# A conformer block on one core: a new order of the instruction blocks and new PSUM banks, from a re-timing in which ScalarE's operations end later

## The chip, the cores and the metric

The kernel runs on one core of a Trainium2 chip. The metric is the device time of one execution in microseconds (us). A core has five engines that run their own instruction streams in order and meet only through semaphores: TensorE (PE in the profile; PEld is its weight load), VectorE (DVE), ScalarE (ACT), GpSimd (POOL) and SyncE (SP, which here only issues DMAs). Matrix products land in PSUM, which this kernel uses as eight banks of 512 fp32 columns.

## The reference

The input x has shape (2, 4000, 144): two sequences of 4000 tokens. The reference is one conformer block:

```python
h = layernorm(x);  x = x + 0.5 * (silu(h @ w_ff1a) @ w_ff1b)        # 144 -> 576 -> 144
h = layernorm(x);  q, k, v = split(h @ w_qkv)                        # 4 heads of 36
p = softmax(q @ k.T * 36**-0.5);  x = x + (p @ v) @ w_o              # full attention, 4000 x 4000
h = layernorm(x) @ w_pw1;  h = h[:, :144] * sigmoid(h[:, 144:])      # gated linear unit
c = depthwise convolution of h along the tokens, 5 taps
x = x + silu(c) @ w_pw2
h = layernorm(x);  x = x + 0.5 * (silu(h @ w_ff2a) @ w_ff2b)
return layernorm(x)
```

Nearly all of the work is the attention: 2 x 4 x 4000 x 4000 exponentials.

## The kernel before, in words

**Tiling.** The 8000 tokens are cut into 16 chunks of 500, eight for each sequence. The keys of a sequence are cut into 62 tiles of 64 and one of 32. One attention tile is one chunk of queries against one tile of keys for all four heads: a 128 x 1000 block of scores in two neighbouring PSUM banks. There are 16 x 63 = 1008 such tiles.

**One attention tile.** `emit_S` (line 1783) puts the scores on TensorE: eight 64 x 64 matmuls over 500 columns into a pair of banks out of the six banks 0 to 5. `emit_exp` (line 1797) then lets ScalarE take the exponential of all 1000 columns at once and write it as bf16 to one of 15 SBUF buffers (PT); with that the pair of banks is free again. `emit_O` (line 1866) multiplies the result with the values and adds it up in banks 6 and 7. For 190 of the 1008 tiles `dve_tile` (line 1811) does the exponential on VectorE with integer arithmetic: two operations read the scores from PSUM, each freeing one bank, and three more finish the tile in SBUF.

**The work around it.** Each chunk also goes through a front part (layer norm, first feed-forward in `ff_tile` at line 1208, the q, k and v projections) and a back part (`epilogue`, output projection, gated unit, convolution, second feed-forward, last layer norm and the store, in `post2` at line 1629). Their PSUM results come from the same six banks. Layer norm statistics are taken on VectorE, the power -0.5 on GpSimd, the normalised rows mostly on GpSimd, and they are transposed by VectorE and by DMAs through a scratch tensor `rows`. Inside the attention, silu is made of a tanh on ScalarE (TH) and a product on VectorE (HT, U, SW). The first 40 us or so and the last 40 us are without the full stream of attention tiles: there the chunks' own chains of dependent steps stand alone.

**What sets the order.** A planner in the kernel (class `Rec`, with the scheduler `Sched` and `pick`) first records all operations in an order that comes from an estimate of their durations. It is the same in both kernels. Operations that one call records on one engine are a block. Then `Rec.reorder(ORDER)` (line 281, called at line 2115) moves the blocks: for each of the five engines the table `ORDER` (line 38) has one letter for each block, which says by how many places it moves up or down in that engine's queue. `PLACES` (line 111) holds one digit for each PSUM tile: the bank, or the first of the pair, which it uses. `Rec.place` reads it. After that, `reorder` works out which tile of a bank follows which in TensorE's order, and makes the first matmul of the later one wait for the readers of the earlier one. So both tables act on waits, not only on positions. `Rec.replay` (line 409) issues everything; all instructions therefore have line L419 in the profile, and only their tiles tell them apart.

The moving itself is these lines of `reorder`:

```python
shift.append(c - 45)
...
at[i + shift[i]] = blk
...
lines[e] = [o for blk in at for o in blk]
```

Of the kernel before, what the change touches and what calls it, by code (L numbers as in the profile page):

```python
# [39 lines left out]
        "PPPPPPPPQOPPPPROQNPPQRPQLPPRPTPUPNIZOVOKVVL~OOKOK~OUHINSNLMMMOPNOJSOOL[I[KMYMKOGRNJHFKOOOE^NNN_dMKLM"  # L40
        "nXMJ@LJMFMYGaJNKMJhLLLLljKKKKKKWKMMWNKK`BJJJQRecHFSIGKH]QKMRGKPMJJMMQTNPNXTRSUJUJJJSLPMPPQUQQNKOTOOR"
        "OQLPPPPPYOOPN[NNNOMfRNLYULMIMOS^KIMOJNaNNQMNHPPaUOMQNYKPSPPQUSVV^QQ^_Q5<@QCPMKIMNNTQMSMNSNUOYQKMMOQQ"
        "^MSOORNOPPCOORPZP^O]OOO[OCNOQEHMUJNNTOMR[MQWXMPMMNNDMPXSNNZMMTMMMTMPLMPP]OOOOQQNUKNOMQMP]WNOMPNVKYPN"
        "JNQHNOOPQQQMPPQOPUP]MNNNOOTNNOMNWOPPMPNOW]VNN[MMHMKYMMQ]YKI`JLQYJJKV[KHMJTLJOJPMQORPVMQNYMN]MN[bLLLL"
        "LMNLPRPKWOYFMNOVNOHXXMKOLNNNN[[_MMMTLLTKKKLJOOPRP`MO_OMNOMPQLLMRMMMPPPQOSYP[MOOISOLNPPIPSPTOLRNNWPNO"
        "QQMMPUQRN[QQQRJFPPPPJQQSPPKQQNPPPPVPPQOPVXOOPNDNPRROSVSYNFWMPYUPNDPJFPNPTOPYOLOPNQ[NLNRPMRLNNOPhUNZM"
        "MMNLNNPMMWYLPNZKNLMF[LPPSLVINLNOMWQNYPYPLQHKOSNORPGPPPS[OOLOOPPYLNNNVOMNOM^QMNTOO_KMMNOMPPLPNQOYL]RY"
        "LMKLMMPLY]KLNNQXMRXSLI[MDObNOENPMMNSNNQMMWNNNOSVNiKZNNQOTFNNOMXXUMMMM?TLLIYMQXXLLMMQZMJJ`ORLMUMKQYNL"
        "INPMMUVNLNOMYPMOORNNRUNKPNO_ROQLSSKMQMKPROLPSOORNOSOOOTVNNNNSNTMTMNNOVXNOMORLSNVXIMSYLMKLN^XYNLMNHMM"
        "WLLMXMNYMOLNNXMNXMMVMM[SLJLLZN^OLNNJUbLLLQNLPRGNNOOOPNRNOPPPeOOOOPSOOORROf`OPNO^@QDLJLMOLTKLTMTRKGMQ"  # L50
        "QNUOPNROYYPZOHNbILLLLbTLLSLLLLPLM_M[MMMMMcMMMMNLMOdZMNNNNIMMMMXMNNVOMKMMZNOUaMMMQMM]^HOMKNNNJZMKM[LM"
# [31 lines left out]
    "dve": (
        "PUO[VM~P6~P6~P)~P6ILIKKLDKMJQRJJJKIKQKKLJKMKOLJWOILJHLJNQNPHFGNNNJMMMMBMWOIKIMINLMNOODNDPSPLORCFVSWC"
        "JDJSIOMBREEMKNCMMMMFNNJMMMMMMNLOPSPROLPPRPNPQOQOQQQMQOQQNPQQNQOPPQOPPQOPPPQOROOPROQVQOYPNOPROSPXURVQ"
        "UU;JNIQQSSSOSQRSSZRSSSKRVQUJ=OO)PROQNPRPRSLPRPQJQOPPPUOPNPQ`VPVOVOMEULFNKNRMRPQQQQIQOPQOQOSOORNTNOPN"
        "QOPQOPPQOQOPPPRPNPROQRMQRPQRPTPPPRPVVPNPSOLQQQQQQ5PPVPPPPPQRHQQQLPPPPPPPPQOPPPPPPPPPROSNPNPPPQSQSLSO"
        "RJQQLQQQQQQQQHPPROSPPTRPNQGQOPQOUQOPLQNRPNPQORUNNOOQNSOOTRUOMTOOPFPQOPPPPPPQQRRRKMRPNPQOPPPPPPPPPPQR"
        "PRPQQQHQOPWOPSOSKTLVOSNUNQMDOPPROOSOPNSQO^PjOOOSNNNCMNTMPLMNTNNNNNOOOPROOROOPRPQQRPJPRSNNQNPQOQOPQOQ"
        "OYRNNNYNOMNSOLRMULQNNOTPPMOQOQOPQOPPPSOPNSOSNPQLPPPPPPPVOOOOOXNOOROQNKUOOOOQNQOPPTTPNLNPPPPPPPPPPQSP"  # L90
        "PLQOPPP]OOOOOOOOOOOOQOQOPQOQOROOPQOWOPNOOOORPNPSPNSSPRSJTJWMRSLLRLMPTRNNQQLQOPPPPPPPPPQQSMPNPRPSPPQJ"
        "PPPPPQQNPQOQQNQOROOPQOPPPRPNPPPQQNPPPPTOOOOPQOPRPNQOQQRSOKQNQOSOOQNQRNOPQOSQRMMPPPPPROQNQOPPPPPQOPPP"
        "PQRPQRRORPQFPPPPPPPPPWPNPNOOOUPNOPNQSNSNNSNORNUQMPMOPROOROVNOOOPQMPPPPPPXQNQMQUNQNSOUQQUCOJOOPPQQNQO"
        "PPUPNOOOPPQRPQQRJQTPLOOTOOOOPPPQVNOQTMQNSQTNTFNNQNQOPPQQNPQOPPPQOQORPSPLOTOOOORORNQSMSNTRPRJRPIROQNQ"
        "OPTQNNTNOOSNSNNOUOOOOOPPPPPPROOROOQOQUROQSUSTGOHKPPPPPQOPQOQOPPQOPPROOQOPPPPPPPPPQRPUPPSORTRPRSUURXS"
        "=KQAQRNQQEPPPPPPPQOQOSOSOhTPMPRMSEOOKOPPPPPPROGNOPPPQRNRNOPQQQMPPPPPQQNQQNQQQQQKQQQRVOXOHOOLOOQNRPNP"
        "PPPPPPPSOOWNSNNQMUQKSOOQJQUN^PhLNKOPPKOKNNNPPMOOOOOOOOQQQRRKNPRPRPSQOQTPTODNRNQNQQUPLPROTRPWMXSNPSQW"
        "RZQUFOSDO7KOPPPTOOSOTOPPIPPPQOPPPPPPTPQMQMPQOPQQNQQRRORRRUQRPUWTQNRSCTRPRRRRDQQRPSPRSQR[RTQNPREO~NKO"
        "RNaNOOOPQMNQYNOPNPTQFNJPRRNNPPPPQOPQOPUPPPPSQOVVFNNNNNPPROOPPPPPROQNPPQQNPPRORPUPTQINLPPQOQOPPPPQOQQ"
        "RMTPPROUQRPFLQRNOPPROOUOXNNNUMNVWL[PRVIGPIOINQNPQQRTUSOITJPKOPSQS`PQQRHRSSTVSWWGRGW<FHMWWMVLLMTMKLO"  # L100
    ),
    "pool": (
        "PPPPPPPROOPPPSOPNPQQQQQQJPPPPPP_PPPPPJOOPQ[NKTMMOMNOSNUMNSNRNTKVNVMPLMPMROQTMOOTVMNNNOQTMOOQXMOOOTNN"
        "OMPPQOPPUOQNNOPPQOPQQNROO"
    ),
    "sp": (
        "PPQOPPPPQOPPPPPPPPPPPPPPWPWMNNNOPLPPPPPPQOPPPPPQRNOPPPPPQOPPQOPPPPPPPPPPPPPPPPPPPPPPPTOPNYNOWNNNNNNN"
        "VOWNNNNPMOPVOZNOMNNOOSNNNPPZOPNOOOOOOOPXOOOOOPPQLPPPPPPQO"
    ),
# [2037 lines left out]
```

## Time and profile before

| | us |
|---|---|
| median of 3 runs | 875.85 |
| lowest and highest | 875.37, 875.96 |
| profiled execution, its own time | 875.47 |
| its span, first to last instruction | 873.7 |
| TensorE busy | 844.9 |
| VectorE busy | 825.3 |
| ScalarE busy | 845.2 |
| GpSimd busy | 294.8 |

Three engines are busy for 94 to 97% of the span, so the share of busy time alone does not name the bound. Two things help in reading it. Operations on ScalarE overlap: the next one starts before the last one has written its result, so busy time can hide short delays, and the distance from start to start tells more than the duration. And TensorE's busy time holds pipelined matmuls with modelled ends, so a busy TensorE may have room.

### The profile page before, as it was taken

The page shows a single profiled execution, that of the slowest core. Times are in us where ns is not written, and L with a number is a line of the kernel's source. Part 1 is how long each engine was busy: PE and PEld are TensorE (multiplying, and loading weights), DVE is VectorE, ACT ScalarE, POOL GpSimd, SP SyncE. Part 2 cuts the span into 40 slices and gives each one's busy share as a digit, 9 for nine tenths or more (in the row PEclk, how much of TensorE's full clock was granted, in tenths as well). Part 3 has the DMA queues.
Part 4 walks back from the last instruction along what each step waited for, and adds up shares of the span by engine and source line. Part 5 has one row for each costly group of instructions (what it writes and reads, how often), then busy time and mean ns, then how long its engine had stood idle before and what let it go on. Part 6 is the DMA issues. An engine that isn't in the chain of part 4 may idle for free.

```text
span 873.7 us, 27060 instructions
## 1 busy us (share of the span) xinstructions
PE 844.9 (97%) x11419; PEld 385.8 (44%) x11419; DVE 825.3 (94%) x1821; ACT 845.2 (97%) x1098; POOL 294.8 (34%) x573
## 2 busy tenths in 40 slices
PE   8999999999999999999999999999999999999996
PEld 6543444334444434443444444445434433444466
DVE  8978999999999999999989999899999999999987
ACT  6799999999999999999999999999999999999985
POOL 6650450341325141152211552621414413022433
PEclk9999999999999999999999999999999999999999
DMA  4221101121121020212001120110111011001111
GB/s 100 51 57 32 24 17 43 35 66 31 27 53 39 16 51 11 44 22 48 21 4 29 24 56 17 31 29 16 38 31 25 20 31 21 18 15 37 25 29 35
DMA packets 114353, 28.82 MB, mean 33 GB/s; under 512 B 101090, under 2 KB 114230, under 8 KB 114230
## 3 DMA queue, kind: packets, MB, share of 16 engines
q1 hardware_dynamic: 112646, 26.39, 13.9%
q8 instruction: 90, 1.47, 0.7%
q10 hardware_dynamic: 1584, 0.69, 0.3%
q14 instruction: 33, 0.27, 0.1%
HBM read 13.44 MB, written 13.61 MB: 31 GB/s over the span
## 4 chain that ended last, share of the span: by engine, by line
ACT 65%; PE 20%; DVE 11%; POOL 3%; issue 1%; POOLq 0%; ACTq 0%
ACT PT L419 60%; PE PS L419 20%; ACT TH L419 5%; DVE PT L419 4%; DVE ST L419 2%; DVE XN L419 2%; POOL XN L419 1%; DVE X L419 1%; POOL RS L419 1%; DVE HT L419 1%; DVE RS L419 0%; DVE AN L419 0%; DVE U L419 0%; DVE KT L419 0%; DVE XT L419 0%
## 5 line engine op out<-in xcount | busy, mean ns | idle before, releaser
L419 ACT ACTIVATE PT<-PS 128x1000 bf16<-128x1000 f32 (+1 forms) x818 | 751.6, 1050 | 3.4 <-PE PS L419 2.8
L419 PE MATMUL PS<-QT,KT 64*64 64x500 bf16 x3968 | 419.4, 384 | 12.2 <-ACT PT L419 7.4
L419 PE MATMUL PS<-PT,VA 64*37 64x500 bf16 x4728 | 406.5, 372 | 1.8 <-DVE QT L419 1.0
L419 DVE TENSOR_SCALAR PT<-PS 128x500 int16<-128x500 f32 x380 | 250.7, 670 | 7.5 <-PE PS L419 5.7
L419 PEld LDWEIGHTS PS<-QT,KT 64*64 64x64 bf16 x3968 | 124.6, 104 | 230.4 <-ACT PT L419 130.3
L419 POOL TENSOR_SCALAR RS<-ST 125x4 f32<-125x4 f32 x130 | 38.3, 295 | 473.8 <-DVE ST L419 467.2
L419 PEld LDWEIGHTS PS<-PT,VA 64*37 64x37 bf16 x4728 | 142.4, 96 | 94.9 <-issue 14.1
L419 DVE TENSOR_SCALAR PT<-PT 128x1000 uint16<-128x1000 uint16 x380 | 154.7, 421 | 2.3 <-PE PS L419 1.0
L419 POOL TENSOR_SCALAR XN<-X,RS 125x144 bf16<-125x144 bf16 x260 | 144.9, 587 | 9.6 <-DMA out_dram<-XN 1.5
L419 DVE TENSOR_TENSOR PT<-PT 128x1000 bf16<-128x1000 bf16 x190 | 127.6, 675 | 0.8
L419 ACT ACTIVATE TH<-PS 128x500 bf16<-128x500 f32 (+3 forms) x194 | 102.3, 550 | 5.2 <-PE PS L419 5.2
L419 POOL TENSOR_TENSOR RS<-RS,NHALF 125x4 f32<-125x4 f32 (+2 forms) x93 | 93.9, 1013 | 33.6 <-DVE RS L419 28.1
L419 DVE SCALAR_TENSOR_TENSOR HT<-TH,PS 128x500 bf16<-128x500 bf16 (+1 forms) x135 | 81.2, 614 | 8.4 <-ACT TH L419 7.8
L419 PE MATMUL PS<-XT,WA 128*128 128x500 bf16 (+4 forms) x288 | 75.6, 368 | 3.4 <-DVE PT L419 0.8
L419 DVE BATCH_NORM_STATS2 ST<-X 125x6 f32<-125x288 bf16 x160 | 65.8, 447 | 1.6 <-DMA X<-in_x_dram 1.2
L419 DVE SCALAR_TENSOR_TENSOR X<-PS,X 125x288 bf16<-125x288 f32 x128 | 56.7, 450 | 4.9 <-PE PS L419 3.6
L419 PE MATMUL PS<-WB,HT 128*125 128x144 bf16 (+1 forms) x640 | 52.8, 230 | 0.6 <-ACT HT L419 0.2
L419 PEld LDWEIGHTS PS<-WB,HT 128*125 128x125 bf16 (+1 forms) x640 | 44.4, 136 | 13.9 <-issue 4.3
L419 PEld LDWEIGHTS PS<-XT,WA 128*128 128x128 bf16 (+1 forms) x288 | 21.4, 98 | 36.4 <-issue 10.3
L419 POOL COPY U<-U 128x2 bf16<-128x2 bf16 (+1 forms) x54 | 12.2, 266 | 56.2 <-DVE U L419 56.2
L419 DVE STREAM_TRANSPOSE XN<-XN 128x320 f32<-128x320 f32 x54 | 27.0, 501 | 4.0 <-POOL XN L419 4.0
L419 PE MATMUL PS<-U,DG 128*128 128x250 bf16 (+6 forms) x204 | 27.8, 263 | 0.1
(95 smaller groups left out, 521.0 us busy)
## 6 DMA issues: line engine op xcount, KB each, us to landing
rows<-XN SPq DMA_DIRECT2D x216, 40.0 KB, 2.0
XT<-rows SPq DMA_DIRECT2D x56, 128.0 KB, 2.0
rows<-AN SPq DMA_DIRECT2D x60, 40.0 KB, 2.0
X<-in_x_dram SPq DMA_DIRECT2D x15, 140.6 KB
XTQ<-rows SPq DMA_DIRECT2D x26, 70.3 KB
out_dram<-XN SPq DMA_DIRECT2D x13, 140.6 KB
XT<-rows SPq DMA_DIRECT2D x56, 16.0 KB, 1.9
out_dram<-XN SPq DMA_DIRECT2D x3, 70.3 KB
```

The costliest lines, as they stand in the source:

```text
L419: ins = getattr(eng, o.name)(*o.a, **o.k)
```

## The change

Both tables are replaced: `ORDER` and `PLACES`. All other lines are the same; so are all instructions, their shapes and their engines. The new tables come from a re-timing of the whole schedule in which ScalarE's operations end later than was assumed for the tables before, by what the trace shows.

Against the order before, on TensorE 8637 of 11419 instructions stand at another position (10 places away on average), on ScalarE 178 of 1106 (its DMA issues counted), on VectorE 1118 of 1821, on GpSimd 417 of 569, and 160 of SyncE's 466 DMA issues. Of 1724 PSUM tiles 254 are in another bank or pair.

The diff, cut to the first lines of some tables:

```diff
 ORDER = {
     "pe": (
-        "PPPPPPPPQOPPPPROQNPPQRPQLPPRPTPUPNIZOVOKVVL~OOKOK~OUHINSNLMMMOPNOJSOOL[I[KMYMKOGRNJHFKOOOE^NNN_dMKLM"
-        "nXMJ@LJMFMYGaJNKMJhLLLLljKKKKKKWKMMWNKK`BJJJQRecHFSIGKH]QKMRGKPMJJMMQTNPNXTRSUJUJJJSLPMPPQUQQNKOTOOR"
...
+        "PPPPPPPPQOPPPQOSPNOPQRPQLPPRPSPSQNI[XNOMQVLyLPI~OYKINRNLMMOOLOPNSOOH[J[KLYNKOHRNLHHKPNP@VOOOYdNLMNo["
+        "MKAMKMHLZLbIMIMIbLLLLiZJKKKKKXKNNXcGK^BKKKT[fMHHQKFHKfRLMSFLOMKQMMSLNNNXUMMXLLPMKSNNNPPUQRPMKSSNNUPV"
...
     "dve": (
-        "PUO[VM~P6~P6~P)~P6ILIKKLDKMJQRJJJKIKQKKLJKMKOLJWOILJHLJNQNPHFGNNNJMMMMBMWOIKIMINLMNOODNDPSPLORCFVSWC"
...
+        "PQQXZL~P)~P1~P5~P6KKKKKKDKKMKLOKKKMRJKKLJKMKOLJSMIMKHLJROMNHHHLNNJMMMMFMWOIKIMINLMOOODNDPRPLQSBFWSXC"
...
 PLACES = (
-    "3054320451505435202310543130213550204405323242301405230054110122532155431241204124012410314032034023"
...
+    "0410325144131405212310543130013550014415323302142105230054110123532155431241204124012410124032034023"
...
```

More of the change, by code (lines that the diff above doesn't have):

```diff
@@ new lines @@
+        "LMKPQRL[PPPPJOOOOOOPPROXNOOSNNNRTOPROQVTOOOOASOOQNXTWMNLZLOZUPNIPNDQO]UOPTOLBQNKOOROSQMNUOOOP]MO[NNN"
+        "NNTMOLLUYKOMOR]KXTZKURMKEGJKScMNQMQWWOLPHLNRMOROFPPPQSPPLPPQQZMOOPNOVNNNTMNN_PMZUMMMNLNYKNLP[UJTYNKK"
+        "HLXORL[RHKMMQWMTXNLIZMJNaMMYMOLLMYMMXLM[MMMNREMiQYMMPNZFMMNLXVKLLLLU^LLOGLQX[LLMMMPLPKaSULLPMKZMSNLM"
+        "NLQaTKKNOMPPMOOPQMRUNKPNOdQOQLPTRKOMKOPNOOXNNPMOQNNPXRNNNOPNUNZNNNNaPNOKOQLPMS]_OTTINHKQWNDIMNVOLOWN"
+        "NNTNN]MMOOO`NNVNNKMMYTMKNLXM]JMOOKX]RLJPMKVXGLNUKLLNTMQNNPeObNNORNNNQQNYaNOMN^?`CJJPMJUMJLUKPTKHMQQM"
@@ new lines @@
+        "WOPNOO[[RVNNJ[GLLLL[WKMULLLNXJLZMQMMYLMdMMMMPMMOdXMMMOMKMMMMXXMMYMMJNKRJN^VLOMQMMM^XOMKMMNYNNKN[MMRa"
+        "LLLNWMMMMYSLLLWbLPHMXTMGNKMTLXL[KLLcTMK]ZMJRGbKOLZIMMRAORKSMCLNPPRR_NLOOOPNWNOVLMMMMSUMUMMN`bLMbMMMM"
+        "MMMMNLNNPNYOGNWXNLOLNKROQKYaNOPNKQOLLOQQNQOXP]GNNOPNSXNNGOLOOOPXOOOOOOWOMWPNXKMMOZLOOLQQ[LLOMPPMeQdN"
+        "KPNPdMNNNNhQL?K_MIMHNINNKUNTVIKMKOHWOOOOVSYLSXKLTYKELY^KIMMMMNcMM_MMMMNOMSbMKMKLMXLNRMMeLLNO^JehLLRM"
+        "KIOYJbIFK`JGQIKKK[MaDKKLLcKLQNKKNNNNNSNNNNSYNOKSNN]NLNOOTPMPQKL]QQN[QJPMOPIMNOOPPhOPRMOPROWNTOMN`RTA"
@@ new lines @@
+        "OPPPPPPPROOPPSUNNNOQQMPPPPPPPQOQOPQOPPPPPPPPPPQOPPPPPPPPPPPQOPPPPPPPPPPQOPPPPQOQOPPPPRPNPQOPPQOQOQOQ"
+        "OPPRPNQOPPPPPPPPPPPPPPPPPPPPPPPPPPPPPPQRNOPRPQMPPPPPPPQQNPPPPPPPPPPPPPPPPPQOPPPPQOPPPPPPPPPPQOQOPPPP"
+        "PPPQOQOPPPPPPPPPPPPPPPPPQOPPPPPPQOPQQNPPPPPPPPPPPPPPPPPPPPTOOPNPPPPPPPPPQQNPPPPPPPPQOPPPPPRPNPPPPPPQ"
+        "OQOPPPPPPPPPPQRNOQOPPPPPPPQOPPPPPPPPPPPPQOPPQOPPPPPPPPPPPPPPPPPPPPPPPPPPPPPPPPPPPPPPPPPPPPPPPPPPPPPP"
+        "PPPPPPPPPPPPPPPQOPQOPPPPPPQOPPSOOTNPNRPRX_JMPMOLQMMOVNNOMOSNOOQOPQSPSOKOPSTTMNLNPPXQOPPKOOQN"
@@ L104 @@
[L104 removed]
+        "PPPPPPPQOPPPPSPNOPPPPQQQMQOPPPP[OOOOOSNNNPaLSQNLYLNNSMRLLTKWJNSXLOLPKOSNPMRUNPPTQJMOPQTNOOOQXNPPMPPP"
+        "QKPPPPPPSOOOPROOROOPROQN"
     ),
     "sp": (
[L107 to L108 removed]
+        "PPQOPPPPQOPPPPPPPPPPPPPPWQVMMNNOQLPSOOOPPQOPQOPQSNOOPPPPQOPPROOQOPPPPPROOPPPPPQOQOPPPVOPNWNNVMNNNNOP"
+        "UOWNNNNPNOPUOTNOMNPPPUOOOOOYQQMMOOOOOPPUYNNNNNOOOOPPPPQQN"
@@ new lines @@
+    "0245042504250235042504250425042504250425042504243023502430342035301430254320452042042504240525053205"
+    "2405420532052450240524052504250425042505250424053205240452203404203103215541240314210412041204131043"
+    "1034205320530515301030153502350523024302430243014301430243023501340243034203420134031340142034120402"
+    "1402140214021402140134143134021402140214021401340104312042104310431043104012430145301140124240214204"
+    "1214021402140210420041204120412041202423003423502431043024302421342503034021402142104214124021402140"
@@ new lines @@
+    "2140214021401340214020412040214031041204120412140134013402140204120402141124021402015240250425042052"
+    "4035023505240243010402342034120524120412040214020412041204120412412411034013402143425301503510351341"
+    "0401401342035320340134013402140120430253205301530153015301301035024310043214031530130104320430243014"
+    "1350235024302430243103502350230232042402340234203410431340135301530153015031503513513214301530134031"
+    "0431410420411043104301352035013403104310412043134013403104120412041204120431040214120423502430342024"
@@ L130 @@
+    "2034203420342034302402340234034030343421053103410430234022402504240524025040254214302430420425052024"
+    "3502350524042020420552054204520225043504320524052042505240524020532504523042321420040342034203420340"
+    "2532043104203420243024202430243024024310341042304302401530240324023203502350243024303240214021421412"
+    "0412041200412142043104024012411340104021401240210143502045312346410441340065523032142105143240214533"
+    "554032042015135102146143"
 )
```

113 lines of the change are left out of this document (41 added, 72 removed).

## The prediction

> **What bounds the kernel now.** I read the busy times first, then the chain of work that ended last, then the busy time by stretch.
>
> ```profile
> span 873.7 us, 27060 instructions
> ...
> PE 844.9 (97%) x11419; PEld 385.8 (44%) x11419; DVE 825.3 (94%) x1821; ACT 845.2 (97%) x1098; POOL 294.8 (34%) x573
> ...
> ACT 65%; PE 20%; DVE 11%; POOL 3%; issue 1%; POOLq 0%; ACTq 0%
> ```
>
> ```profile
> core 0: us, PE busy (x) PEld busy (x) DVE busy (x) ACT busy (x) POOL busy (x), PEclk, DMA share, GB/s
> 0.00:60.00 60.00, 55.55 (x612) 33.77 (x613) 52.02 (x152) 47.44 (x82) 41.83 (x94) 0.97 0.31 70
> 60.00:836.00 776.00, 758.48 (x10463) 327.28 (x10462) 742.79 (x1565) 772.59 (x955) 238.79 (x454) 1.00 0.14 30
> 836.00:868.00 32.00, 30.91 (x346) 24.77 (x346) 28.92 (x101) 24.06 (x61) 12.88 (x25) 1.00 0.10 26
> 868.00:873.70 5.70, 0.00 (x0) 0.00 (x0) 1.57 (x6) 1.13 (x3) 1.35 (x2) 0.62 0.17 47
> ```
>
> The second row is the attention: ScalarE is busy for 772.59 of 776 us, VectorE for 742.79, and 65% of the chain runs over ScalarE. The first and third rows, the start and the last three chunks, leave ScalarE idle for 12.6 and 7.9 us; there the chain is VectorE's and TensorE's.
>
> ScalarE's busy time is not its shortest time, since successive operations overlap. A stretch of its time order shows the distance from start to start:
>
> ```profile
> 413.49 2.87 ACT L419 ACTIVATE PT<-PS 128x1000 bf16<-128x1000 f32 x3
> 416.14 0.69 ACT L419 ACTIVATE TH<-PS 128x500 bf16<-128x500 f32 x1
> 416.61 6.50 ACT L419 ACTIVATE PT<-PS 128x1000 bf16<-128x1000 f32 x7
> 422.96 0.63 ACT L419 ACTIVATE TH<-PS 128x500 bf16<-128x500 f32 x1
> ...
> 424.31 0.45 ACT L419 ACTIVATE TH<-PS 128x250 bf16<-128x250 f32 x1
> 424.61 1.05 ACT L419 ACTIVATE PT<-PS 128x1000 bf16<-128x1000 f32 x1
> ```
>
> Three exponentials take 416.14 - 413.49 = 2.65 us, 0.883 us each, where nothing holds them. The next seven take 6.35 us, 0.907 each: 0.17 us of waiting that busy time hides. A 500-wide tanh takes 0.47, a 250-wide one 0.30. The groups of ScalarE between 60 and 836 us are:
>
> ```profile
> L419 ACT ACTIVATE PT<-PS 128x1000 bf16<-128x1000 f32 x782 | 724.8, 1059 | 2.6 <-PE PS L419 2.0
> L419 ACT ACTIVATE TH<-PS 128x500 bf16<-128x500 f32 x109 | 68.0, 638 | 0.8 <-PE PS L419 0.8
> L419 ACT ACTIVATE PT<-PS 128x500 bf16<-128x500 f32 x15 | 9.9, 663 | 0.0
> L419 ACT ACTIVATE TH<-PS 128x250 bf16<-128x250 f32 x20 | 9.3, 465 | 0.0
> L419 ACT ACTIVATE TH<-PS 64x125 bf16<-64x125 f32 x15 | 4.4, 296 | 0.0
> L419 ACT ACTIVATE TH<-PS 80x125 bf16<-80x125 f32 x13 | 3.8, 289 | 0.0
> L419 ACT ACTIVATE KT<-PS 128x500 bf16<-128x500 f32 x1 | 0.6, 615 | 0.0
> ```
>
> At their shortest distances: 782 x 0.883 = 690.5; the 125 operations of 500 columns x 0.47 = 58.8; 20 x 0.30 = 6.0; the 28 small ones at 0.12 (their mean less the 0.17 by which an exponential's mean of 1.059 exceeds its distance) = 3.4. Together 758.7 us. So 776 - 758.7 = 17.3 us, 2% of the time, is all that any order can win on ScalarE here; the profile's page counts 3.4 us of it as idle, the rest hides in the overlap.
>
> [...]
>
> **The change, part by part.** No instruction is added or removed, and ScalarE's own order hardly moves. What can change is how late the scores come, what TensorE's queue holds ahead of them, and how VectorE is fed. I counted this in the two orders.
>
> *Room before ScalarE's operations.* For each one fed by TensorE I take the last ScalarE operation whose end TensorE must see before the scores, and the TensorE work from that waiter to the end of the scores. Room is ScalarE's work in between less that work and less 0.28 us for the signals. TensorE's price is from these rows:
>
> ```profile
> 400.99 0.38 PE L419 MATMUL PS<-QT,KT 64*64 64x500 bf16 x4
> 401.20 0.38 PE L419 MATMUL PS<-PT,VA 64*37 64x500 bf16 x4
> 401.58 0.11 PEld L419 LDWEIGHTS PS<-QT,KT 64*64 64x64 bf16 x4 [0.48 <-ACT PT L419]
> 401.58 0.41 PE L419 MATMUL PS<-QT,KT 64*64 64x500 bf16 x4
> ```
>
> Four packed matmuls go in 401.20 - 400.99 = 0.21 us. (The last two are scores whose weight load waited 0.48 us for a bank of ScalarE, with the rest of the queue behind it.) Under 0.3 us of room had 102 of 946 operations before and have 87 after, 15% fewer: the intended effect is there. Its price lies between 15% of all 17.3 us (-2.6) and 0. Visible waits for scores are 2.0 + 0.8 = 2.8 us, and 15% of them is -0.4. I take -0.4: some 550 operations stand at 0.3 to 0.4 in both orders, and most of the hidden 13.9 us must be spread over them in pieces of hundredths.
>
> *Banks.* The pair of scores reuses the banks of the exponential two places before in 545 of 818 tiles, and in 540 after. In one case (at about 505 us) it now follows directly on the exponential before it, where none did. Then scores cannot run under that exponential: the last row prices four of the eight matmuls at 0.41, so with the signal +0.5 us; ends 0 and +0.6.
>
> *Feeding VectorE.* The same count for VectorE's operations fed by TensorE, with its own releases: under 0.3 us of room had 183 of 793, and have 234 after, 28% more. These are its waits for TensorE between 60 and 836 us:
>
> ```profile
> DVE PT L419 <- PE PS L419: 6.7, 19, 0.7
> ...
> DVE X L419 <- PE PS L419: 3.2, 9, 0.9
> ...
> DVE QT L419 <- PE PS L419: 1.5, 3, 1.2
> DVE RD L419 <- PE PS L419: 1.5, 4, 0.6
> ...
> DVE VA L419 <- PE PS L419: 1.1, 3, 0.7
> ```
>
> 28% of 14.0 us is +3.9. It costs nothing if VectorE's idle 33.2 us of the 776 cover it. They do so only where the chain is on ScalarE, and 35% of the chain is not: +1.4. But a late VectorE operation also holds its bank, and the scores for ScalarE stand behind the next user of that bank on TensorE's queue. That speaks for all of it. No row lies nearer to one of these two, so I take their middle, +2.6, and keep 0 and +3.9 as ends.
>
> *GpSimd and SyncE.* GpSimd's copies at the chunk edges move past whole groups of layer norm work, some by 100 us in the trace's terms. They cost nothing as long as the convolution that reads them comes later still, which it does in the new order; GpSimd's own waits are for work to arrive:
>
> ```profile
> POOL RS L419 <- DVE ST L419: 467.2, 41, 42.5
> ...
> PEld PS L419 <- DMA XT<-rows: 1.4, 4, 0.5
> ```
>
> Without that cover TensorE would stand behind a convolution. The 160 moved DMA issues pass layer norm rows and loads of x; TensorE waited 1.4 us in all for such data, so 0, with ends of -1.4 and +1.4.
>
> *The start.* Five clears of VectorE move into the gap before x lands, and TensorE swaps projections of the first two chunks. The first row's clock of 0.97 over 60 us is 1.8 us of lost clock; a filled or a new gap is worth that much, so I take 0 between -1.8 and +1.8.
>
> *The end.* From 836 us on, VectorE's order of the last three chunks is mixed anew (some steps by 10 us). It is busy for 28.92 of 32 us, so its work sets the length; its idle 3.1 us bound the gain, and I let as much more be the loss. Only the last steps can be read:
>
> ```profile
> 868.75 0.17 DVE L419 TENSOR_SCALAR RS<-ST 125x2 f32<-125x2 f32 x1
> 868.84 0.71 DVE L419 TENSOR_SCALAR XN<-X,ST,RS 125x144 bf16<-125x144 bf16 x2
> 869.74 0.16 DVE L419 SCALAR_TENSOR_TENSOR RS<-ST,RS 125x2 f32<-125x2 f32 x1 [0.20 <-POOL RS L419]
> ```
>
> ```profile
> 869.00 0.71 POOL L419 TENSOR_TENSOR RS<-RS,NHALF 125x2 f32<-125x2 f32 x1 [0.36 <-DVE RS L419]
> ```
>
> ```profile
> 869.94 0.90 ACT L419 ACTIVATE XN<-X,RS 125x144 bf16<-125x144 bf16 x2 [1.71 <-DVE RS L419]
> ```
>
> Now the last statistics (868.92) go through GpSimd to 869.71, VectorE's 0.16 and ScalarE's 0.90: 870.84. After, the half that ends last is normalised by VectorE itself: 0.08 + 0.70 for GpSimd and 0.71, from the same 868.92 as the work before it is the same: 870.4. That is -0.4, between -3.1 and +3.1.
>
> **The sum.** -0.4 + 0.5 + 2.6 + 0 + 0 - 0.4 = +2.3 us, on the profiled execution's 875.47 (span 873.7 and 1.8 around it): 877.8. That execution is 0.4 us under the median of 875.85; against the median I forecast +0.2%.
>
> **The rivals.** A measurement of this kernel can tell about 0.2% (1.75 us) from no change.
>
> *Faster: VectorE's idle time covers its waits.* Then +2.6 falls to 0 and ScalarE keeps its gain. For it: 65% of the chain is ScalarE's, and VectorE's 33.2 us. Against: 35% is not. Halfway between the small and the full gain on ScalarE (-1.5), with half of the start's 1.8 and the -0.4 of the end, it gives -2.8: 872.7; at the ends 870.7. It decides once less than about 0.3 us of VectorE's added waits reach the chain.
>
> *No change.* If ScalarE's 0.927 (724.8 / 782) were its shortest distance, a new order could win nothing, and the new waits would be hidden under it: 875.5. The 0.883 speaks against it. [...] It is also what comes out if gains and losses cancel.
>
> *Slower by the end alone.* VectorE's mixed order lets it run dry in the last three chunks, since a step of one half now stands ahead of a ready step of another: its idle time there doubles, +3.1, and the attention stays as it is: 878.6. For it: six halves share one queue. Against: TensorE is busy for 30.91 of 32 us there and feeds all of them.
>
> **How the numbers follow.** Slower by VectorE's feeding 0.33 (877.8; its own range 877 to 883, with the new waits, the end and the start all at their costs), slower by the end 0.12, faster 0.33, no change 0.22. The first and third are close; I hold the first for likeliest to come out, by the larger of the two changes in the counts (28% more against 15% fewer). So slower 0.45, within 0.2% 0.22, faster 0.33. The lowest sum of the ends is 875.5 - 2.6 - 0.4 - 1.8 = 870.7, the highest 875.5 + 0.6 + 3.9 + 1.8 + 3.1 = 884.9; 871 to 883 leaves out no more than 2 in 10.
>
> **What would show it.** Right: between 60 and 836 us the sum of VectorE's waits for TensorE grows from 14 to about 18 us, ScalarE's waits for scores stay near 2.8 us or fall a little, the stretch of the attention ends about 2 us later, and the last statistics are normalised by VectorE. Wrong: VectorE's waits grow and the attention ends no later (they were covered), or the distance of the exponentials falls from 0.927 by more than 0.003 (2.3 us over 782), or the time moves before 60 or after 836 us.

## The result, and the profile after

The changed kernel takes 881.75 us (median of 5 runs, 879.46 to 882.41), the kernel before 875.72 in the same session (875.04 to 875.96): a ratio of 1.0063, 95% interval 1.0047 to 1.008. So it is slower by 6.0 us where +2.3 was forecast, and its runs spread over 2.95 us where those of before spread over 0.92. The profiled execution is one of 881.75 us.

The page's lines on the span, the busy times and the shares of the chain, for the changed kernel:

```profile
span 879.6 us, 27051 instructions
...
PE 847.7 (96%) x11419; PEld 384.8 (44%) x11419; DVE 826.0 (94%) x1821; ACT 845.8 (96%) x1098; POOL 295.5 (34%) x573
...
ACT 57%; PE 25%; DVE 9%; POOL 3%; DMA 2%; issue 1%; SPq 1%; POOLq 0%; DVEq 0%
```

The same work by stretch, in the columns of the prediction; the attention now ends near 842 us:

```profile
0.00:60.00 60.00, 54.60 (x599) 33.19 (x599) 51.25 (x150) 46.13 (x81) 41.06 (x93) 1.00 0.29 68
60.00:842.00 782.00, 763.85 (x10498) 327.05 (x10498) 744.52 (x1567) 775.24 (x958) 242.05 (x461) 1.00 0.14 30
842.00:874.00 32.00, 29.28 (x328) 24.52 (x328) 28.79 (x100) 23.53 (x59) 11.73 (x20) 1.00 0.11 28
874.00:879.70 5.70, 0.00 (x0) 0.00 (x0) 1.44 (x6) 0.90 (x2) 0.70 (x1) 0.54 0.21 61
```

Work is the same to a few us; idle time has grown. DMA and SyncE, which had no share of the chain before, have 2% and 1% of it. A mean over the attention does not say where. What does is the start of each exponential of 1000 columns against the one of the same ordinal before (802 in both):

| | shift, us |
|---|---|
| first (before: 18.75 us) | +1.26 |
| the one before at 179.40 | +1.32 |
| the one before at 192.66 | +4.86 |
| the last (before: 835.36) | +4.57 |
| end of the span | +5.96 |

So 1.26 us are lost before 20 us, 3.54 between 179 and 193, 1.39 after the last exponential, and the long rest of the attention gives back 0.2. Three places, then. (These are shifts between two profiles; how far one profile can be trusted for the start, e5 shows below.)

**The read.** SyncE's queue around 177 us, first of the kernel before, then of the changed one. XT<-rows are the reads of transposed rows (two DMAs each, of 128 and 16 KB), X<-in_x_dram the loads of x for later chunks, 140.6 KB each:

```profile
177.15 1.08 SPq L419 DMA_DIRECT2D XT<-rows  x2
178.27 0.34 SPq L419 DMA_DIRECT2D X<-in_x_dram  x1
178.65 0.81 SPq L419 DMA_DIRECT2D XT<-rows  x2
179.50 0.70 SPq L419 DMA_DIRECT2D X<-in_x_dram  x2
```

```profile
177.45 0.82 SPq L419 DMA_DIRECT2D XT<-rows  x2
178.31 0.71 SPq L419 DMA_DIRECT2D X<-in_x_dram  x2
179.06 0.83 SPq L419 DMA_DIRECT2D XT<-rows  x2
179.93 0.32 SPq L419 DMA_DIRECT2D X<-in_x_dram  x1
```

Two blocks of SyncE have changed places. The read that the gated unit's projection needs (queue t1) was first and is now second, behind the other read and two loads. The changed kernel's chain around it (start, us, what):

```profile
177.45 0.35 SPq L419
...
179.06 0.35 SPq L419
...
179.46 4.68 DMA XT<-rows
...
184.18 5.88 PE PS L419 x46
```

And that matmul on TensorE's time order, of before and of after, with the idle time ahead of it:

```profile
180.11 0.62 PE L419 MATMUL PS<-XT,WP 128*128 128x500 bf16 x2
```

```profile
184.18 0.63 PE L419 MATMUL PS<-XT,WP 128*128 128x500 bf16 x2 [2.54 <-DMA XT<-rows]
```

Before, the read's second half was issued at 177.81 and landed at 179.68, 1.87 us later and 0.43 us ahead of its matmul. After, it is issued at 179.46 and takes 4.68. TensorE issues nothing else for 2.54 us, the scores of the attention stand behind that matmul in its order, and ScalarE and VectorE run dry after it. The stretches of 2 us from 180 us on show that, and one thing more in the column PEclk (the granted clock, third from the end):

```profile
180.00:182.00 2.00, 1.64 (x32) 0.64 (x24) 2.00 (x5) 2.00 (x3) 1.61 (x3) 1.00 0.64 130
182.00:184.00 2.00, 0.00 (x0) 0.00 (x0) 0.85 (x3) 0.63 (x1) 1.94 (x4) 1.00 0.37 130
184.00:186.00 2.00, 1.82 (x14) 0.42 (x14) 0.72 (x2) 0.87 (x2) 0.43 (x1) 0.73 0.08 27
186.00:188.00 2.00, 2.00 (x24) 1.29 (x24) 1.17 (x3) 1.35 (x3) 0.00 (x0) 0.50 0.00 0
188.00:190.00 2.00, 2.00 (x25) 0.76 (x15) 1.85 (x4) 1.95 (x3) 0.00 (x0) 0.92 0.00 0
```

After the gap the granted clock is 0.73, 0.50 and 0.92 in the three stretches from 184 to 190 us, and ScalarE is busy for only 0.87 and 1.35 of 2 us in the first two of them, while TensorE is busy for 1.82 and 2.00.

**The start.** VectorE's time order from the landing of x, of before and of after:

```profile
3.81 0.46 DVE L419 BATCH_NORM_STATS2 ST<-X 125x6 f32<-125x288 bf16 x1 [1.21 <-DMA X<-in_x_dram]
...
4.51 0.10 DVE L419 TENSOR_SCALAR RS<-ST 125x2 f32<-125x2 f32 x1
...
4.86 0.40 DVE L419 BATCH_NORM_STATS2 ST<-X 125x6 f32<-125x288 bf16 x1
...
5.45 0.69 DVE L419 TENSOR_SCALAR XN<-X,ST,RS 125x144 bf16<-125x144 bf16 x2
```

```profile
3.73 0.46 DVE L419 BATCH_NORM_STATS2 ST<-X 125x6 f32<-125x288 bf16 x1 [0.47 <-DMA X<-in_x_dram]
4.75 0.46 DVE L419 BATCH_NORM_STATS2 ST<-X 125x6 f32<-125x288 bf16 x1 [0.55 <-DMA X<-in_x_dram]
5.13 0.29 DVE L419 TENSOR_SCALAR RS<-ST 125x2 f32<-125x2 f32 x2
6.12 1.57 DVE L419 TENSOR_SCALAR XN<-X,ST,RS 125x144 bf16<-125x144 bf16 x4 [0.70 <-POOL RS L419]
```

Before, the small RS operation of the first half stood between the two statistics; now it stands behind the second, which waits for the second half of x. GpSimd gets the first half's RS 0.6 us later, and the first normalisation starts at 6.12 instead of 5.45.

**The end.** The last steps, on VectorE and on ScalarE with its DMA queue, of after:

```profile
874.74 0.17 DVE L419 TENSOR_SCALAR RS<-ST 125x2 f32<-125x2 f32 x1
...
875.72 0.54 DVE L419 TENSOR_SCALAR XN<-X,ST,RS 125x144 bf16<-125x144 bf16 x2 [0.75 <-POOL RS L419]
```

```profile
875.00 0.90 ACT L419 ACTIVATE XN<-X,RS 125x144 bf16<-125x144 bf16 x2 [2.94 <-DVE RS L419]
876.29 0.26 ACTq L419 DMA_DIRECT2D out_dram<-XN  x1
```

From the last statistics (874.91) to the last normalised half (876.26) it takes 1.35 us; the prediction's rows of before give 1.92 (868.92 to 870.84). But the statistics themselves come later, and the last store, issued at 876.29, is done only at 879.6: 3.3 us, where before one of nearly the same size was issued at 870.87 and done at 873.7, 2.8 us.

### The profile page after: what moved, and what is told of

Same layout as the page of the kernel before. It is cut to its first block, busy times and chain, and to the rows that moved or that the text cites. A ratio compares the mean times of both kernels' runs of the same rounds, so it can differ in the third digit from the quotient of the medians.

```text
span 879.6 us, 27051 instructions
## 1 busy us (share of the span) xinstructions
PE 847.7 (96%) x11419; PEld 384.8 (44%) x11419; DVE 826.0 (94%) x1821; ACT 845.8 (96%) x1098; POOL 295.5 (34%) x573
## 4 chain that ended last, share of the span: by engine, by line
ACT 57%; PE 25%; DVE 9%; POOL 3%; DMA 2%; issue 1%; SPq 1%; POOLq 0%; DVEq 0%
ACT PT L419 53%; PE PS L419 25%; ACT TH L419 5%; DVE PT L419 3%; POOL RS L419 2%; POOL XN L419 2%; DVE ST L419 1%; DVE XN L419 1%; DVE HT L419 1%; SPq L419 1%; DVE X L419 1%; DMA XT<-rows 1%; DMA rows<-XN 0%; DMA X<-in_x_dram 0%; DVE KT L419 0%
## 5 line engine op out<-in xcount | busy, mean ns | idle before, releaser
L419 ACT ACTIVATE PT<-PS 128x1000 bf16<-128x1000 f32 (+1 forms) x818 | 751.4, 1066 | 4.6 <-PE PS L419 3.9
L419 PE MATMUL PS<-QT,KT 64*64 64x500 bf16 x3968 | 420.6, 385 | 13.1 <-ACT PT L419 6.9
L419 PE MATMUL PS<-PT,VA 64*37 64x500 bf16 x4728 | 402.9, 372 | 0.7 <-DVE QT L419 0.4
L419 DVE TENSOR_SCALAR PT<-PS 128x500 int16<-128x500 f32 x380 | 250.1, 670 | 12.4 <-PE PS L419 10.3
L419 PEld LDWEIGHTS PS<-QT,KT 64*64 64x64 bf16 x3968 | 124.7, 104 | 245.1 <-ACT PT L419 136.3
L419 POOL TENSOR_SCALAR RS<-ST 125x4 f32<-125x4 f32 x130 | 37.5, 289 | 475.8 <-DVE ST L419 469.4
L419 PEld LDWEIGHTS PS<-PT,VA 64*37 64x37 bf16 x4728 | 141.6, 96 | 85.7 <-issue 8.6
L419 POOL TENSOR_SCALAR XN<-X,RS 125x144 bf16<-125x144 bf16 x260 | 152.2, 615 | 8.3
L419 DVE TENSOR_SCALAR PT<-PT 128x1000 uint16<-128x1000 uint16 x380 | 152.6, 417 | 1.1
L419 DVE TENSOR_TENSOR PT<-PT 128x1000 bf16<-128x1000 bf16 x190 | 127.0, 673 | 0.6
L419 ACT ACTIVATE TH<-PS 128x500 bf16<-128x500 f32 (+3 forms) x194 | 103.7, 564 | 8.0 <-PE PS L419 6.1
L419 POOL TENSOR_TENSOR RS<-RS,NHALF 125x4 f32<-125x4 f32 (+2 forms) x93 | 89.6, 967 | 36.2 <-DVE RS L419 30.7
L419 DVE SCALAR_TENSOR_TENSOR HT<-TH,PS 128x500 bf16<-128x500 bf16 (+1 forms) x135 | 80.5, 615 | 6.6 <-ACT TH L419 6.1
L419 PE MATMUL PS<-XT,WA 80*128 80x500 bf16 (+5 forms) x288 | 75.2, 364 | 2.7 <-DVE XT L419 0.8
L419 DVE BATCH_NORM_STATS2 ST<-X 125x6 f32<-125x288 bf16 (+1 forms) x160 | 65.7, 447 | 1.4 <-DMA X<-in_x_dram 1.0
L419 DVE SCALAR_TENSOR_TENSOR X<-PS,X 125x288 bf16<-125x288 f32 x128 | 56.8, 450 | 5.6 <-PE PS L419 4.7
L419 PE MATMUL PS<-WB,HT 128*125 128x144 bf16 (+1 forms) x640 | 52.5, 230 | 0.6 <-ACT HT L419 0.3
L419 PEld LDWEIGHTS PS<-WB,HT 128*125 128x125 bf16 (+1 forms) x640 | 44.4, 136 | 14.0 <-DVE PT L419 3.7
L419 PEld LDWEIGHTS PS<-XT,WA 128*128 128x128 bf16 (+1 forms) x288 | 21.2, 97 | 33.9 <-issue 8.9
L419 DVE STREAM_TRANSPOSE XN<-XN 128x320 f32<-128x320 f32 x54 | 27.1, 502 | 3.9 <-POOL XN L419 3.4
L419 POOL COPY U<-U 128x2 bf16<-128x2 bf16 (+1 forms) x54 | 10.5, 234 | 58.7 <-DVE U L419 58.7
L419 PE MATMUL PS<-U,DG 128*128 128x250 bf16 (+6 forms) x204 | 28.0, 263 | 0.5
## 6 DMA issues: line engine op xcount, KB each, us to landing
X<-in_x_dram SPq DMA_DIRECT2D x15, 140.6 KB
XTQ<-rows SPq DMA_DIRECT2D x26, 70.3 KB
out_dram<-XN SPq DMA_DIRECT2D x13, 140.6 KB
out_dram<-XN SPq DMA_DIRECT2D x3, 70.3 KB
```

The costliest lines, as they stand in the source:

```text
L419: ins = getattr(eng, o.name)(*o.a, **o.k)
```

## The experiments

Two theories stand against each other. The first: the loss is in those three places, and the new order of the attention costs nothing in sum. The second, the prediction's: VectorE is starved through the attention; the three places are only where it shows. (The recorded expectations below name a theory A and a theory B of their own each time.) In the tables a letter is the shift of a block of instructions, so an exchange of two blocks is two pairs of letters, and a stretch of another order means many lines; of these the diffs show a few. The kernel before took 875.6 to 875.7 us beside all of them.

**e1: SyncE's two blocks back in their old order.**

```diff
 # after, ORDER["sp"]
-        "PPQOPPPPQOPPPPPPPPPPPPPPWQVMMNNOQLPSOOOPPQOPQOPQSNOOPPPPQOPPROOQOPPPPPROOPPPPPQOQOPPPVOPNWNNVMNNNNOP"
+        "PPQOPPPPQOPPPPPPPPPPPPPPWQWMMNNOPLPSOOOPPQOPQOPQSNOOPPPPQOPPROOQOPPPPPROOPPPPPQOQOPPPVOPNWNNVMNNNNOP"
```

> The changed kernel with two neighbouring blocks of SyncE's queue exchanged, nothing else: the read of the transposed rows for the gated unit (cid t1, followed by one load of x) goes ahead of the read for the feed-forward and its two loads of x, as it stood before the change. Theory A (the read is late because two loads of x of 140.6 KB were issued just ahead of it and TensorE's queue stops for it at 181.6 to 184.2 us): TensorE's wait for XT there goes, the 30 exponentials after it come 3 us earlier, time 878.4 (877.5 to 879.5). Theory B (the stretch is longer because VectorE and TensorE were fed with less room in the new order, and the late read is only where that shows): at most 0.5 us of change, 881.2 to 881.8.

878.47 us (877.12 to 879.44), ratio 1.003 [1.002, 1.004]: 3.3 us of the 6.0 are gone with one exchange in one queue of DMA issues. The read lands 1.86 us after its issue, TensorE does not wait for it, and the exponentials keep a shift of 1.23 us at the first, 1.13 at 192 and 0.53 at the last.

**e2: the same exchange, made in the kernel before.**

```diff
 # before, ORDER["sp"]
-        "PPQOPPPPQOPPPPPPPPPPPPPPWPWMNNNOPLPPPPPPQOPPPPPQRNOPPPPPQOPPQOPPPPPPPPPPPPPPPPPPPPPPPTOPNYNOWNNNNNNN"
+        "PPQOPPPPQOPPPPPPPPPPPPPPWPVMNNNOQLPPPPPPQOPPPPPQRNOPPPPPQOPPQOPPPPPPPPPPPPPPPPPPPPPPPTOPNYNOWNNNNNNN"
```

> The kernel before with the same two blocks of SyncE's queue exchanged the other way, so that the gated unit's read stands behind two loads of x as in the changed kernel; no other engine's order is touched. Theory A: the read lands some 4 us later than its 179.7 us, TensorE asks for it at 180.1, so the kernel before becomes 3 us slower: 878.5 to 879.5. Theory B: no change, 875.4 to 876.2.

881.91 us, ratio 1.0076 [1.0062, 1.0089]: the exchange alone makes the kernel before as slow as the changed one, 6.2 us, twice what I had expected. Here the read lands only at 183.99 (3.99 us after its issue) and its matmul would have been due 1.6 us sooner than in the changed kernel:

```profile
184.03 0.62 PE L419 MATMUL PS<-XT,WP 128*128 128x500 bf16 x2 [4.03 <-DMA XT<-rows]
```

The exponentials shift by 5.15 us there, 1.1 more than the wait, again with a halved clock (0.50 from 186 to 188 us).

**e7 and e8: is it the place in the queue, or the loads ahead?** e7 leaves the two reads in the new order, but moves the two loads of x behind the second; e8 moves the same two loads ahead of the first read in the kernel before.

```diff
 # e7: after (e8: before, with the loads put at the index of "x13" - 2)
             lines[e] = [o for blk in at for o in blk]
+        s = lines["sp"]
+        late = [o for o in s if o.q in ("x12", "x14")]
+        s = [o for o in s if o not in late]
+        k = [o.q for o in s].index("x13")
+        lines["sp"] = s[:k] + late + s[k:]
```

> The new kernel with the two loads of x that stand ahead of the gated unit's read moved behind it; the other read stays ahead of it. Theory A (the read lands late because 281 KB of loads stand ahead of it on the queues): issued 0.75 us earlier, it lands 2.0 to 2.5 us after its issue instead of 4.7, TensorE waits at most 0.5 us for it, 878.5 to 879 us. Theory B (it is late because it stands behind the other read, whose rows are written late): TensorE's wait shrinks by the 0.75 us of the two issues alone, to about 1.7 us, and the time stays at 880.5 us or above.

> The kernel before with only the same two loads of x moved ahead of the gated unit's read; the reads keep their order. Theory A: the read is issued 0.75 us later and lands over 4 us after its issue instead of 2.3, TensorE waits 2 to 4.5 us for it, 878.5 to 881 us. Theory B: the read lands 2.3 us after its issue, TensorE waits 0.5 us at most, 875.7 to 876.3 us.

e7: 878.83 us, ratio 1.0032 [1.002, 1.0045]. TensorE no longer waits for the read, which is issued at 178.75 and lands at 180.54, after 1.79 us. e8: 878.76 us, ratio 1.0031 [1.0019, 1.0042]; the read is issued at 178.49, 0.68 us later than before, and lands at 182.53, after 4.04 us. SyncE's queue in e7, and TensorE's waits of e8 from 172 to 195 us (five added lines of code make L419 to L424):

```profile
177.43 1.75 SPq L424 DMA_DIRECT2D XT<-rows  x4
179.22 1.09 SPq L424 DMA_DIRECT2D X<-in_x_dram  x3
```

```profile
PEld PS L424 <- DMA XT<-rows: 2.4, 1, 2.4
...
PE PS L424 <- DMA XT<-rows: 2.0, 1, 2.0
```

It is the loads. In all profiles the 16 KB half of this read lands 1.8 to 1.9 us after its issue with no load ahead of it (1.87 in before, 1.86 in e1, 1.79 in e7) and 4.0 to 4.7 with two (4.68 in the changed kernel, 3.99 in e2, 4.04 in e8). The place behind the other read alone costs its 0.8 us of issue, for which TensorE does not wait in e7. How the two loads hold the read up on its way, no run shows.

**e3: before's order and banks up to 60 us, the new ones from there.**

```diff
 # after; ORDER and PLACES, cut
 PLACES = (
-    "0410325144131405212310543130013550014415323302142105230054110123532155431241204124012410124032034023"
+    "3054320451505435202310543130213550204405323242301405230054110122532155431241204124012410314032034023"
...
```

> The changed kernel with the old order and the old banks for everything that started before 60 us in the kernel before. If the start's loss is a place of its own (exponentials are 1.2 us late from the first one on), it comes back whole: 880.5 (880.0 to 881.0), with the stall near 181 us and the end unchanged. If the later stretches absorb an earlier start (the late read sets the time at 184 us whatever came before it), nothing comes back before the read and the time stays at 881.5 to 882.

880.52 us, ratio 1.0056 [1.0043, 1.0068]: 1.2 us less than the changed kernel, as the first exponential showed; but both kernels' runs spread over 2 us or more and their intervals overlap, so this run alone does not prove the price. In the profiled execution, the fastest of the five, TensorE waits 2.00 us for the read, and its clock holds:

```profile
182.00:184.00 2.00, 2.00 (x26) 0.92 (x30) 1.06 (x2) 1.39 (x2) 0.72 (x2) 1.00 0.04 16
184.00:186.00 2.00, 1.80 (x22) 0.48 (x14) 1.96 (x6) 2.00 (x4) 0.00 (x0) 1.00 0.00 0
```

**e5: e1, and VectorE's RS of the first half ahead of the second statistics.**

```diff
 # e1's kernel, ORDER["dve"]
-        "PQQXZL~P)~P1~P5~P6KKKKKKDKKMKLOKKKMRJKKLJKMKOLJSMIMKHLJROMNHHHLNNJMMMMFMWOIKIMINLMOOODNDPRPLQSBFWSXC"
+        "PQQXZL~P)~P1~P5~P6KLJKKKDKKMKLOKKKMRJKKLJKMKOLJSMIMKHLJROMNHHHLNNJMMMMFMWOIKIMINLMOOODNDPRPLQSBFWSXC"
```

> The new order with SyncE's two blocks exchanged (the kernel of the first experiment, 878.47 us), and VectorE's reciprocal of the first half of the layer norm put ahead of the statistics that wait for the second half of x. Theory A (the start lost 1.2 us because that one instruction stands behind the wait for x): first exp back from 20.0 to about 18.9 us, 877.4 us. Theory B (the start lost its time to other moves, the five clears or GpSimd's among them): first exp stays at 20.0 us and the time at 878.5 us.

877.57 us, ratio 1.0023 [1.0013, 1.0032], 0.9 less than e1, with intervals that overlap. The first exponential is at 19.34 us, not back at 18.9. But the order of before itself starts it between 18.56 and 19.45 in nine profiles (mean 18.97), and the new order between 19.68 and 20.01 in four (mean 19.91), so one profile cannot say whether a rest is left. By the means the start's loss is 0.9 us rather than 1.26, and the one small instruction gives back 0.6 of it, the larger part as far as this profile shows.

**e4 and e11: the end.** e4 is the changed kernel with before's order and banks from 840 us on; e11 is the kernel before with the new ones from 835 us on.

```diff
 # e4: after, PLACES, cut
-    "0412041200412142043104024012411340104021401240210143502045312346410441340065523032142105143240214533"
-    "554032042015135102146143"
+    "0412041200412142043104024012411340104021401240210143502240540316224455153562430123441101203205424135"
+    "154252140154303532026214"
 # e11: before, PLACES, cut
-    "0412041201412042041204024012412140214021401240214042303250540316224455153562430123441101203205424135"
-    "154252140154303532026214"
+    "0412041201412042041204024012412140214021401240214042303045312346410441340065523032142105143240214533"
+    "554032042015135102146143"
```

> The changed kernel with the old order and the old banks for everything that starts after 840 us in it. From the last exponential to the end the changed kernel takes 35.45 us, the kernel before 34.60. If the new mix of the last three chunks costs that: 0.85 us come back, 880.9 (880.5 to 881.2). If the end is as long because of what is left over at its start: no change, 881.6 to 881.9.

> The kernel before up to 835 us, the new order and banks from there. Theory A (the new end by itself costs 1.4 to 2.6 us, of it 0.8 us from the last exp to the last instruction and the rest in the landing of the last store, which ScalarE issues): 877.1 to 878.3 us, and runs that scatter over more than 1 us. Theory B (the prediction's, the end is worth -0.4 us and what was lost there came with the late attention): 875.3 us.

e4: 879.49 us, ratio 1.0037 [1.0025, 1.005], 2.3 less than the changed kernel. e11: 877.71 us, ratio 1.0024 [1.0015, 1.0033], 2.1 more than the kernel before, in runs that lie 1.8 us apart. So the end is worth about 2 us. The seven profiles with the new end take 1.2 to 2.6 us longer than before from the last exponential to the end of the span; some 0.9 of it goes up to the last instruction, and the rest to its store, which ends 3.2 to 4.6 us after its issue (2.7 to 2.8 in all profiles with the old end).

**e12: e11, its last store issued by SyncE instead of ScalarE.**

```diff
 # e11's kernel, in reorder()
+        o = lines["act"].pop()
+        o.eng = "sp"
+        lines["sp"].append(o)
```

> The kernel of e11 (877.71 us) with its last store, of 69.8 KB, issued by SyncE instead of ScalarE; in the five profiles with the new end it took 3.3 to 4.6 us from the last instruction to the end of the span, in the five with the old end, whose last store is of 70.3 KB and issued by SyncE, 2.8. Theory A (the engine that issues it makes it late): 2.8 us from its issue to the end, 876.3 to 876.6 us. Theory B (the store itself, 124 partitions of 125, makes it late): still 3.3 to 4.6 us, and 877.3 to 878 us.

877.48 us, ratio 1.0019 [1.001, 1.0028], within the scatter of e11, and the store still ends 3.7 us after its issue. So the issuing engine is not the reason. Nor is it the store by itself: with the old end the same 69.8 KB are the last store but one, and in the traces' records of single DMA packets its packets begin 0.8 us after its issue and take 0.9 to 1.2 us. With the new end it is issued 0.36 us behind a store of 70.3 KB, where the last two stores are 1.3 to 1.5 us apart with the old end. Its packets then begin 1.05 to 1.31 us after its issue, while those of the store ahead are still running, in all seven profiles, and take 1.0 to 2.4 us. So the traces show the late store beside another one each time; that this is the cause, and whether the short distance or the 140.6 KB issued 2.4 us ahead matters more, stays argued, as no run took the stores apart.

**e6: only the middle is new** (before's order up to 60 us and from 840 us on, SyncE's exchange as in e1). This is the run that decides between the two theories.

```diff
 # after, cut
     "sp": (
-        "PPQOPPPPQOPPPPPPPPPPPPPPWQVMMNNOQLPSOOOPPQOPQOPQSNOOPPPPQOPPROOQOPPPPPROOPPPPPQOQOPPPVOPNWNNVMNNNNOP"
+        "PPQOPPPPQOPPPPPPPPPPPPPPWQWMMNNOPLPSOOOPPQOPQOPQSNOOPPPPQOPPROOQOPPPPPROOPPPPPQOQOPPPVOPNWNNVMNNNNOP"
...
 PLACES = (
-    "0410325144131405212310543130013550014415323302142105230054110123532155431241204124012410124032034023"
+    "3054320451505435202310543130213550204405323242301405230054110122532155431241204124012410314032034023"
...
-    "554032042015135102146143"
+    "154252140154303532026214"
```

> The order of before up to 60 us and from 840 us on, the new order and banks between them, with SyncE's two blocks exchanged. Theory A (the three places found account for the whole loss, the new order of the attention costs nothing): 875.2 to 875.7 us, last exp within 0.7 us of before. Theory B (the prediction's: a starved VectorE costs some 2.6 us over the attention, only masked by the other losses): 877.5 to 878.5 us.

875.71 us (11 runs), ratio 1.0 [0.9991, 1.0009]. With the three places undone nothing of the 6.0 us is left, to within 0.8 us by the interval, so the first theory holds. VectorE's waits for TensorE in this profile, 60 to 836 us, and two rows of the kernel before that the prediction's sum of 14.0 us leaves out:

```profile
DVE PT L419 <- PE PS L419: 7.6, 23, 0.9
DVE X L419 <- PE PS L419: 3.2, 12, 0.4
DVE QT L419 <- PE PS L419: 1.8, 4, 1.0
DVE VA L419 <- PE PS L419: 1.3, 2, 0.9
DVE RD L419 <- PE PS L419: 1.3, 4, 0.5
DVE KT L419 <- PE PS L419: 0.9, 4, 0.3
```

```profile
DVE U L419 <- PE PS L419: 0.5, 2, 0.3
DVE KT L419 <- PE PS L419: 0.5, 2, 0.2
```

The sum is 16.1 us, against 15.0 before with all rows: VectorE does wait 1.1 us more. Yet from the exponential at 60 us to the last one e6 takes 0.35 us less than before (shifts of -0.37 and -0.72). The waits are covered, or paid back by what ScalarE won; this run measures both together. ScalarE's visible waits for scores hardly changed (2.6 us, 2.8 before), which speaks for covered.

**e9 and e10: can the stretches that win be kept alone?** In e6 the exponentials fall 0.6 us behind between 60 and 160 us, win 1.0 by 490, lose 1.5 up to 560 and win 1.3 of it back by 572. e10 has the new order only from 160 to 500 us, e9 from 160 to 500 and from 573 to 840, both with SyncE's exchange.

```diff
 # e9: e6's kernel, PLACES, cut
-    "4203420340244302402430243203420342040304314023420342034203420342034203420342034203420242034042045012"
+    "4203421340243310402430043213420342040324304023420342034203420342034203420342034203420342024042045012"
...
 # e10: before, PLACES, cut
-    "1402140214021402140134143134021402140214021401340204112042104310431043104012430154301240124240214214"
+    "1402140214021402140134143134021402140214021401340104312042104310431043104012430145301140124240214204"
...
```

> Before's order up to 160 us, the new order and banks from 160 to 500 us with SyncE's two blocks exchanged, before's from 500 to 573, the new from 573 to 840, before's to the end: the kernel of e6 without the stretches where its exps fell behind (60 to 160 us, +0.6 us, and 500 to 560 us, +1.3 us, all but 0.05 of it given back by 572 us). Theory A (the stretches add up): last exp 1.2 us before that of the kernel before, 874.5 us. Theory B (what one stretch wins, the next gives back, since what bounds is the sum of ScalarE's work): last exp within 0.3 us, 875.4 to 875.8 us.

> Before's order and banks, and only from 160 to 500 us the new ones, SyncE's two blocks exchanged. Theory A (the stretches add up): last exp 0.9 us before that of the kernel before, 874.8 us. Theory B: within 0.3 us, 875.4 to 875.8 us.

e9: 875.96 us, ratio 1.0005 [0.9997, 1.0014]. e10: 875.66 us, 0.9998 [0.9989, 1.0007]. The theory A of these two runs, that the stretches add up, fails. Both win 0.6 us from 158 to 458 us and lose 0.4 of it by 499; e9 loses 0.9 more between 560 and 582, where one order joins the other. No kernel tried is faster than the one before.

## Why the prediction was right and wrong

Slower was right, and 881.75 lies inside the range; the size was not (+2.3 for +6.0), and the reason given for it was wrong. So the direction came out by luck: the largest part of the loss sits in a step that the sum put at 0, and the +2.6 that made the forecast positive was not there.

*GpSimd and SyncE: this step failed.* "The 160 moved DMA issues pass layer norm rows and loads of x; TensorE waited 1.4 us in all for such data, so 0, with ends of -1.4 and +1.4." What all reads together made TensorE wait before does not bound what one read can cost after. Needed was the slack of each read that is moved: this one landed 0.43 us ahead of its matmul and was put behind 281 KB of loads, with which it landed 4.0 to 4.7 us after its issue instead of 1.8 to 1.9. e1 prices the step at 3.3 us, over twice its own upper end, and the highest sum of the ends had left even that +1.4 out. e7 and e8 show its cause.

*Feeding VectorE: +2.6 was not there.* The sign that I named did appear. In the changed kernel, 60 to 842 us, the first row of VectorE's waits for TensorE is this one; the other five are as in e6:

```profile
DVE PT L419 <- PE PS L419: 10.3, 25, 2.4
```

They sum to 18.8 us, where "about 18" was to prove it (15.0 before with all rows); and the attention ends later. But 2.8 of them lie in the stretch from 180 to 190 us, the wait for the read passed on (its largest single one is 2.4). A sum over the attention could not tell a starved queue from one late read; e6 could, and there the case "waits grow and the attention ends no later" holds. The count of operations with little room (+28%) had the sign of the waits' growth (+7% in e6), but neither its size nor its price.

*Room before ScalarE and the banks: nearly nothing, as foretold.* The three terms of the attention were to give -0.4 + 0.5 + 2.6 = +2.7 us together; e6 measures -0.35. It does not part them, so that the feeding alone costs 0 is argued from ScalarE's unchanged waits. The exponential at 505 us that follows directly on its own bank waits as priced at +0.5, where before eleven exponentials run in a row without a visible wait. ScalarE's time order in e6:

```profile
500.47 4.57 ACT L419 ACTIVATE PT<-PS 128x1000 bf16<-128x1000 f32 x5
505.55 2.79 ACT L419 ACTIVATE PT<-PS 128x1000 bf16<-128x1000 f32 x3 [0.51 <-PE PS L419]
```

By 572 us that is won back. The new order won next to nothing in sum, though 0.883 us for an exponential had shown that there was something to win. The 0.28 us for the signals in the count of room can be found in the trace of before: an exponential (1.059 us) ends 0.18 us after the earliest start of the next, a weight load of scores that waited for one starts 0.05 us after its end (median of 359), and an exponential that waited for its scores starts 0.05 us after their modelled end (median of ten).

*The start: 0 for +0.9 to +1.3.* The price lay within the ends of 1.8, but I looked for it in the clears and the clock. The first row's clock rose from 0.97 to 1.00, and the start came later all the same. That a gap stands behind the 0.97 was an estimate which the trace does not show: between its first matmul and 22.92 us, where the clock of before is halved, TensorE is idle for 0.51 us at a time at most. For the larger part it was an instruction of 0.1 us put behind one that waits for x.

*The end: -0.4 for about +2.* The half that ends last is indeed normalised by VectorE, and the piece from the last statistics on is 0.57 us shorter. What failed is "the work before it is the same": the instructions up to there come some 0.9 us later in all, and the last store, of which the step says nothing, takes 0.4 to 1.8 us longer.

*The rivals.* The rival "slower by the end alone" had the right place for a third of the loss but another mechanism (an idle VectorE). "No change" described the attention itself, and "faster" had its mechanism, waits that are covered, but not the places outside it.

## What to carry to other kernels

When an order of DMA issues changes, take each read that an in-order engine waits for, and compare its slack before (landing to first use, 0.43 us here) with the bytes that now stand ahead of it in the same queue (281 KB here, with which it landed 4.0 to 4.7 us after its issue instead of 1.8 to 1.9); the sum of the waits before, 1.4 us here, says nothing of it: e2 lost 6.2. A stretch that looks like a slow drift should be laid against the old trace operation by operation first: here 6.2 us sat in three places of 1 to 4 us each, and the order of 800 us in between was worth nothing in sum. And look at what stands behind an instruction that waits for data, however small it is: here an RS operation of 0.1 us, put behind statistics that waited 0.55 us for x, came 0.6 us later, and with it back in its place (e5) the first exponential came 0.6 us before the mean of the new order.

## What the runs showed of the hardware

*TensorE's clock after five gaps: halved after 2.41 us and more, held after 1.97 and 2.00.* TensorE's waits for the read, and what the exponentials lost from 179 to 193 us:

| kernel | TensorE's gap, us | exponentials later by, us | lowest granted clock in 2 us |
|---|---|---|---|
| e8 | 1.97 | 1.88 | 1.00 |
| e3 | 2.00 | 1.81 | 1.00 |
| e4 | 2.41 | 3.35 | 0.50 |
| after | 2.54 | 3.54 | 0.50 |
| e2 | 4.03 | 5.15 | 0.50 |

In the rows up to 2.00 us the loss is a little under the gap, in those from 2.41 us on it is 0.9 to 1.1 more. In the rows of the changed kernel the clock lost from 184 to 190 us is 2 x (0.27 + 0.50 + 0.08) = 1.7 us, that is 3.4 us at half speed: from 184.91 to 188.32 us its mean is 0.50. Five gaps do not settle whether the length decides, at which length, or whether it depends on the moment. Nor does each halving stand behind such a gap: in the profile of before the clock is halved from 22.92 to 26.33 us, 3.41 us as well (the 0.97 of the prediction's first row), with no idle time of TensorE over 0.51 us between its first matmul and there; e11 has the same order there and stays at 1.00, and its exponentials are only 0.3 us earlier for it at 60 us. That the halved clock is what costs the 0.9 to 1.1 us in the attention is read from these rows; no run held the clock up across a gap of 2.4 us or more. It also fits the scatter of the runs: the two of the changed kernel at 879.46 and 879.96 us had a mean granted clock of 0.997, the three from 881.75 us on 0.995, and 0.002 of 880 us is 1.8 us of lost clock.

*The last store took longer with the new end than with the old one:* 2.7 to 2.8 us from its issue to the end of the span in every profile with the old end, 3.2 to 4.6 with the new one, whichever of the two engines issues it. With the old end its packets run alone, in 0.9 to 1.2 us, with the new end beside those of the store issued 0.36 us earlier, in 1.0 to 2.4.
